# Score masks written to PSUM by VectorE, token sums in two halves and a reordered tail in a recurrent attention kernel

## The chip, the cores and the metric

The kernel runs on one core of one Trainium2 chip. The metric is the time of one execution on the device, in microseconds (us); three runs of the kernel before took 779.76, 780.51 and 783.5 us, so its median is 780.51 us. TensorE is the engine for matrix products (in the profile PE, its weight loads PEld), VectorE is DVE, ScalarE is ACT, GpSimd is POOL, and the queue that issues most transfers is SP.

## What is computed

The output is a gated mixture `g * a + (1 - g) * b` of two branches over 2048 tokens of width 512. Branch `b` is a LayerNorm, a GELU layer of 1376 channels and a second layer back to 512. Branch `a` is attention with a memory that is handed from segment to segment. Cut to what matters:

```python
mem = mem0                                   # 8 rows
for s in range(64):                          # segments of 32 tokens
    h = concatenate([mem, x[32*s : 32*s+32]])      # 40 rows
    q, k, v = (einsum('btd,dhe->bhte', h, W) for W in (Wq, Wk, Wv))   # 32 heads of 128
    scores = einsum('bhqe,bhke->bhqk', q, k) * 128 ** -0.5
    scores = where((row < 8) | (row >= col), scores, -1e9)
    o = einsum('bhqk,bhke->bhqe', softmax(scores), v)
    o = einsum('bhte,hed->btd', o, Wo)
    mem = o[:8]                              # the next segment's memory
    outs.append(o[8:])
```

So segment `s + 1` cannot begin its products with `q`, `k` and `v` before the 8 memory rows of segment `s` have gone through attention and `Wo`.

## The kernel before, in words

**First part.** Up to about 98 us the kernel computes branch `b`, loads the four weight matrices of branch `a`, and builds constants. It ends with the first score mask in PSUM. The mask tile `Mk` holds 0 or -1e9 for four heads, 56 columns a head.

**The loop over segments** (64 segments, four to a tile `T` of 128 tokens, the place in the tile is `si`). The order of the work on each engine is written out by hand in the loop body: an engine carries out its instructions in the order of the source. A tile framework adds a wait wherever one engine's instruction touches what another's has to finish first. The PSUM memory is split into eight tiles of one bank each: `U0` to `U3`, `X1`, `X2`, `SbF` and `W`. The body for one segment is:

1. `qk_unit` (L120): products for Q and K in four passes of 16 matmuls into `U0..U3`; each is cast by ACT (L125) and transposed by DVE (L129) into `QT` or `KT`.
2. `scores(s, 0)` (L257, L261): scores of heads 0 to 15 are added to the mask that stands in `SbF`; ACT takes the exponential of all of them into the first half of `E` (L692).
3. Four passes of V into `X1` (L139), then `mask_mm(1)` (L249): four matmuls with an identity matrix that write the mask into `W`. Then the first pass of the second half of V into `X2`.
4. `msum(0)` (L268, L271): eight matmuls that sum the exponentials of the memory rows over the keys, into a free strip of `U0`. `mnorm(0)`: DVE takes the reciprocal (L688) into 32 columns of `SbF`, and multiplies the memory columns of `E` by it (L689).
5. `scores(s, 1)` onto the mask in `W`; ACT takes the exponentials in two pieces (L681), the memory columns first.
6. Two more passes of V, then `msum(1)` and `mnorm(1)` (its reciprocal lies in `W`), then the last pass of V, which ACT copies out (L710).
7. `run(W1)`: filling work (see below). `xsums` (L600): 16 small matmuls that sum the exponentials of the token rows into `SbF`. `recip_x`: DVE takes their reciprocal (L611), SP writes it to memory and reads it back to all partitions, DVE copies the reciprocals of the memory rows out (L617), and POOL adds them to a running sum (L618).
8. `av` (L281, L286): `E` times V for heads 0 to 15, then for heads 16 to 31, into `U0..U3`. ACT copies the memory rows to `UT` (L718) and the token rows to `XR` (L606).
9. `run(W2)`, then `wo_pass` (L151): 32 matmuls with `Wo` into `W`; ACT casts the result in two halves into `w` (L633).
10. `mask_mm(0)` into `SbF`, `run(W3)`, in some segments an output of an earlier tile (`out_sel`), and `new_mem` (L640, L642): the new memory rows, transposed into the next segment's `hT`.

The filling work is a generator of at most eight steps a segment, each four matmuls of 512 columns (Q, K, V or `Wo` of tokens that do not depend on the memory). `WS` says how many steps stand at the places `W1`, `W2` and `W3`: `(3, 2, 0)` for `si` = 0 and `(2, 2, 2)` for the others; one more stands between the two halves of `new_mem`, and what is left behind them.

**The tail.** The last segment takes no new memory. Its token sums go into `SbF` (`sums`, L268 and L271), DVE takes one reciprocal of 256 columns (L746) and multiplies `E` by it, `av` follows, then `wo_left` (32 matmuls, L151), two reductions that look for bad numbers (L763, L764), `wo_pass`, five selection matmuls (L772, L774), one gated sum (L777) and one output transfer (L778).

Of the kernel before, what the change touches and what calls it, by code (L numbers as in the profile page):

```python
# [10 lines left out]
BF16 = mybir.dt.bfloat16  # L11
# [16 lines left out]
def kernel(ctx, tc, A_x, A_mem0, A_Wq, A_Wk, A_Wv, A_Wo, A_seg_len, B_x, B_w1, B_b1, B_w2, B_b2, gate_w, out):  # L28
# [45 lines left out]
    VP = [ep.tile([P, SPT, 2, Dh], BF16, name=f"VP{i}") for i in range(2)]  # L74
    Mk = ep.tile([P, 4, EW], BF16)
    BO = ep.tile([P, P], BF16)
# [169 lines left out]

    def mask_mm(i2):
        for j in range(4):
            nc.tensor.matmul(Sb[i2][32 * j:32 * j + 32], lhsT=ident[:, 32 * j:32 * j + 32], rhs=Mk[:],  # L249
                             start=True, stop=True, skip_group_check=True, tile_position=(0, 32 * j))  # L250

# [40 lines left out]
    with tc.tile_pool(name="mlpw", bufs=1) as mlpw, \  # L292
# [69 lines left out]
        nc.gpsimd.iota(io[:], pattern=[[1, RIDE]], base=0, channel_multiplier=0)  # L362
        nc.gpsimd.memset(Mk[:], 0.0)

# [196 lines left out]

    mask_mm(0)
    Rs = {}
# [27 lines left out]

    xs8 = SbF[:, 256:256 + NG]
    RW = 9 * NG

    def xsums(s, E):

        for first, c0, n in ((True, 8, 32), (False, 0, LEFT)):
            for i in range(NG):
                c, h = i % 4, i // 4
                nc.tensor.matmul(xs8[32 * c:32 * c + n, 4 * h:4 * h + 4], lhsT=E[:, i, c0:c0 + n], rhs=BO[:, 0:P:32],  # L600
                                 start=first and h == 0, stop=not first, skip_group_check=True, tile_position=(0, 32 * c))

# [6 lines left out]
    def recip_x(s):  # L609
        R = Rs.pop(s)  # L610
        nc.vector.reciprocal(out=R[:, 8 * NG:RW], in_=xs8)  # L611

        Rb = cw.tile([P, P, NG], FP32, tag="Rb", bufs=1, name="Rb")
        nc.sync.dma_start(r_dr[s % 2][:], R[:, 8 * NG:RW])
        nc.sync.dma_start(Rb[:].rearrange("p r e -> p (r e)"), r_dr[s % 2][:].rearrange("r e -> (r e)").partition_broadcast(P))
        for i2 in (1, 0):
            nc.vector.tensor_copy(out=R[:, 32 * i2:32 * i2 + 32], in_=RP[i2])  # L617
        nc.gpsimd.tensor_tensor(out=racc[:, 0:RW], in0=racc[:, 0:RW], in1=R[:, 0:RW], op=ALU.add)  # L618
        Rbs[s] = Rb
# [24 lines left out]

    WS = ((3, 2, 0), (2, 2, 2), (2, 2, 2), (2, 2, 2))
    for s in range(nseg):
# [18 lines left out]
        for n, (t, hf) in enumerate(((0, 0), (1, 0), (0, 1), (1, 1))):  # L665
# [27 lines left out]
        for kc in range(KC):  # L693
            v_unit(X1, hc, 0, kc)
        mask_mm(1)
        nc.scalar.copy(out=v_out(V, 0), in_=X1[:])  # L696
# [12 lines left out]
        v_unit(X2, hc, 1, 3)  # L709
        nc.scalar.copy(out=v_out(V, 1), in_=X2[:])  # L710
        if last:
            break
        run(W1)
        xsums(s, E)
        recip_x(s)
# [7 lines left out]
        if s >= 1:  # L723
            ws[s - 1] = w
        mask_mm(0)
        run(W3)
# [15 lines left out]
    sums(xsum, E, 8, 0, 32, True)  # L742
    for _ in out_sel(T - 1, X2):
        pass
    nc.gpsimd.memset(UL[T % 2][:, :, :, LEFT * si:seg], 0.0)
    nc.vector.reciprocal(out=R[:, nx], in_=SbF[:, 0:32 * NG])  # L746
# [8 lines left out]
    flush(dve_q, 9)  # L755
    for _ in wo_left(T, X1):
# [10 lines left out]
    nc.vector.tensor_scalar(out=good[:, 1:2], in0=tot[:, 1:2], scalar1=RSUM_MAX, scalar2=None, op0=ALU.is_lt)  # L767
    wf = wo_pass(UF)
    nc.tensor.matmul(X1[0:1, 0:1], lhsT=good[:, 0:1], rhs=good[:, 1:2], start=True, stop=True)
    bad = okp.tile([1, 1], I32)  # L770
    nc.vector.tensor_scalar(out=bad[:], in0=X1[0:1, 0:1], scalar1=-1.0, scalar2=float(P), op0=ALU.mult, op1=ALU.add)
    nc.tensor.matmul(X2[:], lhsT=SelL[:], rhs=wls.pop(T)[:], start=True, stop=False, skip_group_check=True)  # L772
    for i in range(SPT):
        nc.tensor.matmul(X2[32 * i:32 * i + 32, :], lhsT=(SelR if i < si else SelI)[:], rhs=(ws.pop(SPT * T + i) if i < si else wf)[:],  # L774
                         start=False, stop=True, skip_group_check=True, tile_position=(0, 32 * i))
    o = cw.tile([P, Dm], BF16, tag="o", name="o")
    nc.vector.scalar_tensor_tensor(out=o[:], in0=X2[:], scalar=g_all[:, T:T + 1], in1=cs.pop(T)[:], op0=ALU.mult, op1=ALU.add)  # L777
    nc.sync.dma_start(out2[T * P:(T + 1) * P, :], o[:])  # L778
    man.__exit__(None, None, None)
# [122 lines left out]
```

## Time and profile before

| What | us |
|---|---|
| Runs of the kernel before | 779.76, 780.51, 783.5 (median 780.51) |
| Profiled execution, its own time | 779.49 |
| Its span, first to last instruction | 777.7 |
| PE busy | 761.1 (98% of the span) |
| ACT busy | 529.5 (68%) |
| DVE busy | 345.1 (44%) |
| POOL busy | 278.7 (36%) |
| Mean granted TensorE clock | 0.997 |

The profile is one execution. A row of its timeline gives the start in us from the span's beginning, the duration, the engine, the line of the kernel, the operation, output and inputs with their sizes, and the number of instructions that the row merges; square brackets give how long the engine sat idle before the row and what ended the wait. Matmuls overlap in a pipeline, so a group of matmuls costs TensorE the distance from its start to the start of the next group, not the duration of its row. A view of waits gives, for each pair of waiting and releasing instruction, the total, the number and the longest.

### The profile page before, as it was taken

To read this page: it belongs to the slowest core of one execution; us is meant where nothing else is said; L and a number is where in the kernel's file an instruction comes from. 1 tells how busy PE (TensorE), PEld (TensorE's weight loads), DVE (VectorE), ACT (ScalarE), POOL (GpSimd) and SP (SyncE) were. 2 spreads that over 40 slices of the span, in tenths; PEclk is the share of its full clock that TensorE was granted. 3 is DMA by queue.
4 is the path that set the end of the run, shared out by engine and by line. 5 is a ranking of instruction groups with operands and counts; after the bars stand their busy time and mean duration, and the time that the engine had idled before them with its cause. 6 is when DMAs were issued, how large, how long until landed. Compare 5 with 4: busy or idle time off the path is not lost.

```text
span 777.7 us, 44316 instructions
## 1 busy us (share of the span) xinstructions
PE 761.1 (98%) x19687; PEld 420.3 (54%) x19687; DVE 345.1 (44%) x1235; ACT 529.5 (68%) x1439; POOL 278.7 (36%) x523
## 2 busy tenths in 40 slices
PE   7999999999999999999999999999999999999996
PEld 5666555555555555555555555555555555555553
DVE  5776254344435343434443443534343444444334
ACT  4666576777777677777777677767777777777663
POOL 4111033433443433344433334434324443343342
PEclk9999999999999999999999999999999999999999
DMA  6779412212122222212221212222231212121221
GB/s 195 271 245 390 139 58 62 75 61 79 62 62 71 79 72 68 80 52 72 62 88 61 89 62 56 67 79 72 71 80 58 70 54 88 62 82 62 66 62 48
DMA packets 53174, 70.61 MB, mean 91 GB/s; under 512 B 21289, under 2 KB 42898, under 8 KB 51442
## 3 DMA queue, kind: packets, MB, share of 16 engines
q1 hardware_dynamic: 51250, 64.84, 26.0%
q8 instruction: 156, 2.56, 1.3%
q0 software_dynamic: 784, 1.97, 0.7%
q10 hardware_dynamic: 944, 0.92, 0.3%
q14 instruction: 40, 0.33, 0.1%
HBM read 56.96 MB, written 4.45 MB: 79 GB/s over the span
## 4 chain that ended last, share of the span: by engine, by line
PE 87%; DVE 1%; ACT 0%; issue 0%; DVEq 0%
PE U L120 29%; PE X L139 18%; PE W L151 15%; PE X L120 8%; PE X L151 4%; PE U L281 3%; PE U L640 2%; PE U L268 1%; PE W L257 1%; PE SbF L257 1%; PE W L249 1%; PE SbF L600 1%; PE SbF L249 1%; PE U L286 1%; PE U L466 1%; PE U L221 0%
## 5 line engine op out<-in xcount | busy, mean ns | idle before, releaser
L626 POOL TENSOR_TENSOR UT<-XR,Rb 128x384 bf16<-128x384 bf16 x126 | 140.1, 1133 | 296.2 <-DMA Rb<-r_dr 215.9
L125 ACT CAST Tb<-U 128x512 bf16<-128x512 f32 x258 | 150.8, 585 | 76.3 <-PE U L120 75.3
L120 PEld LDWEIGHTS <-hT 128*32 128x32 bf16 x4096 | 104.6, 96 | 109.3 <-DVE hT L642 16.3
L139 PE MATMUL X<-Wv_sb,hT 128*32 128x512 bf16 x2048 | 151.2, 379 | 0.0
L120 PE MATMUL U<-Wq_sb,hT 128*32 128x512 bf16 x2048 | 133.3, 380 | 0.5 <-DVE hT L642 0.2
L120 PE MATMUL U<-Wk_sb,hT 128*32 128x512 bf16 x2048 | 132.7, 379 | 0.0
L151 PE MATMUL W<-Wo_sb,UT 128*32 128x512 bf16 x2080 | 125.2, 380 | 1.3 <-ACT UT L718 1.2
L642 DVE CAST hT<-U 128x16 bf16<-128x16 f32 x126 | 21.9, 175 | 206.0 <-PE U L640 198.3
L129 DVE STREAM_TRANSPOSE QT<-Tb 128x256 f32<-128x256 f32 x128 | 57.0, 446 | 80.8 <-ACT Tb L125 80.7
L151 PEld LDWEIGHTS <-UT 128*32 128x32 bf16 x2080 | 59.4, 96 | 55.6 <-issue 16.3
L606 ACT CAST XR<-U 128x256 bf16<-128x256 f32 x252 | 78.6, 438 | 0.0
L129 DVE STREAM_TRANSPOSE KT<-Tb 128x256 f32<-128x256 f32 x128 | 57.0, 446 | 46.2 <-ACT Tb L125 46.0
L633 ACT CAST w<-W 128x256 bf16<-128x256 f32 (+1 forms) x128 | 41.9, 378 | 47.3 <-PE W L151 47.3
L626 POOL TENSOR_TENSOR UL<-XR,Rb 128x128 bf16<-128x128 bf16 x126 | 60.4, 503 | 0.0
L618 POOL TENSOR_TENSOR racc<-racc,R 128x72 f32<-128x72 f32 x63 | 21.2, 337 | 107.1 <-PE U L286 75.0
L139 PEld LDWEIGHTS <-hT 128*32 128x32 bf16 x2048 | 48.2, 94 | 21.0
L718 ACT CAST UT<-U 128x64 bf16<-128x64 f32 x252 | 35.3, 227 | 28.3 <-PE U L286 28.3
L710 ACT CAST V<-X 128x512 bf16<-128x512 f32 x64 | 37.4, 585 | 22.5 <-PE X L139 22.5
L466 PE MATMUL U<-w_sb,hTm 128*128 128x512 bf16 (+1 forms) x176 | 52.7, 383 | 0.0
L460 PEld LDWEIGHTS <-w_sb 128*128 128x128 bf16 (+1 forms) x352 | 34.2, 101 | 20.5 <-issue 3.2
L696 ACT CAST V<-X 128x512 bf16<-128x512 f32 x64 | 37.5, 585 | 9.5 <-PE X L139 1.1
L125 ACT CAST Tb<-X 128x512 bf16<-128x512 f32 x62 | 36.9, 595 | 7.8 <-PE X L120 6.0
(159 smaller groups left out, 1168.4 us busy)
## 6 DMA issues: line engine op xcount, KB each, us to landing
Rb<-r_dr SPq DMA_DIRECT2D x63, 512.0 KB, 3.9
Wv_sb<-in_A_Wv_dram SPq DMA_DIRECT2D x4, 1024.0 KB, 7.5
Wq_sb<-in_A_Wq_dram SPq DMA_DIRECT2D x4, 1024.0 KB, 7.2
Wk_sb<-in_A_Wk_dram SPq DMA_DIRECT2D x4, 1024.0 KB, 9.2
Wo_sb<-in_A_Wo_dram SPq DMA_DIRECT2D x4, 1024.0 KB, 15.1
VP<-VL SPq DMA_DIRECT2D x64, 64.0 KB, 3.2
c<-c_dr SPq DMA_DIRECT2D x16, 128.0 KB, 3.2
out_dram<-o SPq DMA_DIRECT2D x16, 128.0 KB, 2.7
```

Source lines behind the costliest of these rows:

```text
L120: nc.tensor.matmul(bk[32 * j:32 * j + 32, :], lhsT=G[:, kc, :], rhs=W5[t][:, kc, h0:h1, j, :], start=(kc == 0), stop=(kc == KC - 1), tile_ ...
L125: nc.scalar.copy(out=Tb[:], in_=bk.rearrange("p (a b e) -> p a e b", a=8, b=2))
L129: nc.vector.transpose(out=dst[:, 8 * hf:8 * hf + 8, c0:c0 + 32, :].rearrange("p a r b -> p a (r b)").bitcast(FP32), in_=Tb[:].rearrange("p ...
L139: nc.tensor.matmul(bk[32 * j:32 * j + 32, :], lhsT=G[:, kc, :], rhs=Wv5[:, kc, 4 * vb:4 * vb + 4, j, :], start=(kc == 0), stop=(kc == KC - ...
L151: nc.tensor.matmul(bk[32 * c:32 * c + 32, :], lhsT=U_[:, j, i, :], rhs=Wo_sb[:, 4 * i + j, :], start=(n == 0), stop=(n == NW - 1), tile_po ...
L466: nc.tensor.matmul(bp(blk, tt)[:], lhsT=hTm[blk % 2][:rows, fc, tt * P:(tt + 1) * P], rhs=w2_sb[:rows, fc, :], start=(fc == 0), stop=(fc = ...
L606: nc.scalar.copy(out=XR[:, j], in_=U[j][:, 0:NG * 40].rearrange("p (i q) -> p i q", q=40)[:, :, 0:32])
L626: nc.gpsimd.tensor_tensor(out=out[:, :, 4 * h:4 * h + 4, o:o + b - a], in0=XR[:, :, 4 * h:4 * h + 4, a:b], in1=Rb[:, h, :, :, a:b], op=ALU ...
L633: nc.scalar.copy(out=w[:, a:a + Dm // parts], in_=W[:, a:a + Dm // parts])
L696: nc.scalar.copy(out=v_out(V, 0), in_=X1[:])
L710: nc.scalar.copy(out=v_out(V, 1), in_=X2[:])
L718: nc.scalar.copy(out=UT[s % 2][:, j, :, 0:M], in_=U[j][:, 0:NG * 40].rearrange("p (i q) -> p i q", q=40)[:, :, 32:40])
```

## The change

Four things change.

- **Masks.** `mask_mm` (four identity matmuls) becomes `mask_put`: a DVE copy from the mask in SBUF to PSUM. `mask_put(1)` (into `W`) stands behind the first transposition of Q; `mask_put(0)` (into `SbF`) at the end of `recip_x`. The mask tile grows by 8 zero columns, which `mask_put(0)` writes too.
- **Token sums in halves.** `xsums` takes a half `h`. The first half is issued right behind `msum(0)` and `mnorm(0)`, ahead of `scores(s, 1)`; the second stays behind `run(W1)`. The sums lie in the 8 columns that the mask copy has set to zero, so no matmul starts an accumulation.
- **Memory-row sums of the second half.** `msum(1)` and `mnorm(1)` stand behind all passes of V. The filling steps for `si` > 0 become `(2, 1, 3)`.
- **Tail.** `out_sel` writes `X1`; three of the eight steps of `wo_left` (into `X2`) come before `wo_pass`; the last `racc` addition moves from POOL to DVE; the selection matmuls, the gated sum and the output transfer are done in two halves of 256 columns, with the matmuls that do not need the last `w` ahead of it.

```diff
-    def mask_mm(i2):
-        for j in range(4):
-            nc.tensor.matmul(Sb[i2][32 * j:32 * j + 32], lhsT=ident[:, 32 * j:32 * j + 32], rhs=Mk[:],
-                             start=True, stop=True, skip_group_check=True, tile_position=(0, 32 * j))
+    def mask_put(i2):
+        c = 4 * EW + (NG if i2 == 0 else 0)
+        nc.vector.tensor_copy(out=(SbF, W)[i2][:, 0:c], in_=MkF[:, 0:c])
...
-    xs8 = SbF[:, 256:256 + NG]
+    xs8 = SbF[:, 4 * EW:4 * EW + NG]
...
-    def xsums(s, E):
-        for first, c0, n in ((True, 8, 32), (False, 0, LEFT)):
-            for i in range(NG):
-                c, h = i % 4, i // 4
-                nc.tensor.matmul(xs8[32 * c:32 * c + n, 4 * h:4 * h + 4], lhsT=E[:, i, c0:c0 + n], rhs=BO[:, 0:P:32],
-                                 start=first and h == 0, stop=not first, skip_group_check=True, tile_position=(0, 32 * c))
+    def xsums(E, h):
+        for c0, n in ((8, 32), (0, LEFT)):
+            for c in range(4):
+                nc.tensor.matmul(xs8[32 * c:32 * c + n, 4 * h:4 * h + 4], lhsT=E[:, 4 * h + c, c0:c0 + n], rhs=BO[:, 0:P:32],
+                                 start=False, stop=True, skip_group_check=True, tile_position=(0, 32 * c))
...
         for i2 in (1, 0):
             nc.vector.tensor_copy(out=R[:, 32 * i2:32 * i2 + 32], in_=RP[i2])
+        mask_put(0)
...
-    WS = ((3, 2, 0), (2, 2, 2), (2, 2, 2), (2, 2, 2))
+    WS = ((3, 2, 0), (2, 1, 3), (2, 1, 3), (2, 1, 3))
...
             qk_tr(qk_cast(bk[:]), (QT, KT)[t], hf, LEFT * (1 - t))
+            if n == 0:
+                mask_put(1)
...
         for kc in range(KC):
             v_unit(X1, hc, 0, kc)
-        mask_mm(1)
         nc.scalar.copy(out=v_out(V, 0), in_=X1[:])
         v_unit(X2, hc, 1, 0)
         if not last:
             msum(0)
             mnorm(0)
+            xsums(E, 0)
         scores(s, 1)
         for i2 in range(2):
             exps(1, i2)
-        for kc in range(1, 3):
+        for kc in range(1, KC):
             v_unit(X2, hc, 1, kc)
-        if not last:
-            msum(1)
-            mnorm(1)
-        v_unit(X2, hc, 1, 3)
         nc.scalar.copy(out=v_out(V, 1), in_=X2[:])
         if last:
             break
+        msum(1)
+        mnorm(1)
         run(W1)
-        xsums(s, E)
+        xsums(E, 1)
         recip_x(s)
         av(s, V, E)
...
-        mask_mm(0)
         run(W3)
...
-    for _ in out_sel(T - 1, X2):
-        pass
     nc.gpsimd.memset(UL[T % 2][:, :, :, LEFT * si:seg], 0.0)
+    for _ in out_sel(T - 1, X1):
+        pass
+    fill = wo_left(T, X2)
+    run(3)
...
-    nc.gpsimd.tensor_tensor(out=racc[:, nx], in0=racc[:, nx], in1=R[:, nx], op=ALU.add)
+    nc.vector.tensor_tensor(out=racc[:, nx], in0=racc[:, nx], in1=R[:, nx], op=ALU.add)
...
-    wf = wo_pass(UF)
+    wf = wo_pass(UF, 2)
+    halves = ((X1, slice(0, Dm // 2)), (X2, slice(Dm // 2, Dm)))
+    for bk, cc in halves:
+        for i in range(SPT):
+            nc.tensor.matmul(bk[32 * i:32 * i + 32, cc], lhsT=SelL[:, 32 * i:32 * i + 32], rhs=wl[:, cc], start=True, stop=False,
+                             skip_group_check=True, tile_position=(0, 32 * i))
+        for i in range(si):
+            nc.tensor.matmul(bk[32 * i:32 * i + 32, cc], lhsT=SelR[:], rhs=ws[SPT * T + i][:, cc], start=False, stop=True,
+                             skip_group_check=True, tile_position=(0, 32 * i))
...
+    for bk, cc in halves:
+        nc.tensor.matmul(bk[32 * si:32 * si + 32, cc], lhsT=SelI[:], rhs=wf[:, cc], start=False, stop=True,
+                         skip_group_check=True, tile_position=(0, 32 * si))
+        nc.vector.scalar_tensor_tensor(out=o[:, cc], in0=bk[:, cc], scalar=g_all[:, T:T + 1], in1=c[:, cc], op0=ALU.mult, op1=ALU.add)
+        nc.sync.dma_start(out2[T * P:(T + 1) * P, cc], o[:, cc])
```

More of the change, by code (lines that the diff above doesn't have):

```diff
@@ L74 @@
     VP = [ep.tile([P, SPT, 2, Dh], BF16, name=f"VP{i}") for i in range(2)]
-    Mk = ep.tile([P, 4, EW], BF16)
+    MkF = ep.tile([P, 4 * EW + NG], BF16)
+    Mk = MkF[:, 0:4 * EW].rearrange("p (a c) -> p a c", c=EW)
     BO = ep.tile([P, P], BF16)
@@ L362 @@
         nc.gpsimd.iota(io[:], pattern=[[1, RIDE]], base=0, channel_multiplier=0)
-        nc.gpsimd.memset(Mk[:], 0.0)
+        nc.gpsimd.memset(MkF[:], 0.0)
         nc.gpsimd.memset(SelM[:], 0.0)
@@ L617, in recip_x @@
             nc.vector.tensor_copy(out=R[:, 32 * i2:32 * i2 + 32], in_=RP[i2])
+        mask_put(0)
         nc.gpsimd.tensor_tensor(out=racc[:, 0:RW], in0=racc[:, 0:RW], in1=R[:, 0:RW], op=ALU.add)
@@ L724 @@
             ws[s - 1] = w
-        mask_mm(0)
         run(W3)
@@ L755 @@
     flush(dve_q, 9)
-    for _ in wo_left(T, X1):
+    for _ in fill:
         pass
@@ L767 @@
     nc.vector.tensor_scalar(out=good[:, 1:2], in0=tot[:, 1:2], scalar1=RSUM_MAX, scalar2=None, op0=ALU.is_lt)
-    wf = wo_pass(UF)
-    nc.tensor.matmul(X1[0:1, 0:1], lhsT=good[:, 0:1], rhs=good[:, 1:2], start=True, stop=True)
-    bad = okp.tile([1, 1], I32)
[L771 to L775, printed above, removed]
-    o = cw.tile([P, Dm], BF16, tag="o", name="o")
-    nc.vector.scalar_tensor_tensor(out=o[:], in0=X2[:], scalar=g_all[:, T:T + 1], in1=cs.pop(T)[:], op0=ALU.mult, op1=ALU.add)
-    nc.sync.dma_start(out2[T * P:(T + 1) * P, :], o[:])
+    wf = wo_pass(UF, 2)
+    wl, c = wls.pop(T), cs.pop(T)
+    halves = ((X1, slice(0, Dm // 2)), (X2, slice(Dm // 2, Dm)))
[6 more added lines that the diff above has]
+                             skip_group_check=True, tile_position=(0, 32 * i))
+    nc.tensor.matmul(U[0][0:1, 0:1], lhsT=good[:, 0:1], rhs=good[:, 1:2], start=True, stop=True)
+    bad = okp.tile([1, 1], I32)
+    nc.vector.tensor_scalar(out=bad[:], in0=U[0][0:1, 0:1], scalar1=-1.0, scalar2=float(P), op0=ALU.mult, op1=ALU.add)
+    o = cw.tile([P, Dm], BF16, tag="o", name="o")
+    for bk, cc in halves:
[3 more added lines that the diff above has]
+        nc.sync.dma_start(out2[T * P:(T + 1) * P, cc], o[:, cc])
     man.__exit__(None, None, None)
```

2 lines of the change are left out of this document (1 added, 1 removed).

## The prediction, made before the changed kernel had run

> **What bounds the kernel now.** I began with the page, which says how much of the span each engine is busy, then went to the timeline of one segment, engine by engine, and last to the waits. The page's span:
>
> ```profile
> span 777.7 us, 44316 instructions
> ```
>
> The page also has TensorE (PE) busy for nearly all of this span, but its rows overlap, so I read the distance from one group's start to the next. Here is PE in a segment with `si` = 1, from the second mask to `wo_pass`:
>
> ```profile
> 406.57 0.27 PE L249 MATMUL W<-Mk,ident 128*32 128x224 bf16 x4
> 406.67 0.39 PE L139 MATMUL X<-Wv_sb,hT 128*32 128x512 bf16 x4
> 406.88 0.19 PE L268 MATMUL U<-E,BO 128*32 128x32 bf16 x4
> 406.91 0.19 PE L271 MATMUL U<-E,BO 128*32 128x32 bf16 x4
> 406.94 0.27 PE L257 MATMUL W<-QT,KT 128*32 128x40 bf16 x16
> 407.04 0.20 PE L261 MATMUL W<-QT,KL 128*32 128x64 bf16 x4
> 407.07 0.63 PE L139 MATMUL X<-Wv_sb,hT 128*32 128x512 bf16 x8
> 407.64 0.20 PE L268 MATMUL U<-E,BO 128*32 128x32 bf16 x4
> 407.67 0.20 PE L271 MATMUL U<-E,BO 128*32 128x32 bf16 x4
> 407.69 0.40 PE L139 MATMUL X<-Wv_sb,hT 128*32 128x512 bf16 x4
> 407.91 0.62 PE L120 MATMUL X<-Wq_sb,GL 128*32 128x512 bf16 x8
> 408.34 0.27 PE L600 MATMUL SbF<-BO,E 128*32 128x4 bf16 x16
> 408.54 0.27 PE L281 MATMUL U<-E,V 32*128 32x40 bf16 x16
> 408.65 0.19 PE L286 MATMUL U<-E,VP 32*128 32x64 bf16 x4
> 408.78 0.27 PE L281 MATMUL U<-E,V 32*128 32x40 bf16 x16
> 408.89 0.19 PE L286 MATMUL U<-E,VP 32*128 32x64 bf16 x4
> 409.02 0.61 PE L120 MATMUL X<-Wq_sb,GL 128*32 128x512 bf16 x8
> 409.49 1.91 PE L151 MATMUL W<-Wo_sb,UT 128*32 128x512 bf16 x32
> ```
>
> Four matmuls of 512 columns cost 0.215 (407.69 to 407.91 for one group, 407.91 to 408.34 for two). The mask at 406.57 costs 0.10. The eight-matmul row of V at 407.07 should cost 0.43, yet the next group starts 0.57 later: PE waits 0.14 before `msum(1)`. `xsums` costs 0.20. Between the two halves of `av` the first half takes 0.24.
>
> VectorE (DVE) and ScalarE (ACT) beside it, first DVE and then ACT:
>
> ```profile
> 406.42 0.45 DVE L129 STREAM_TRANSPOSE KT<-Tb 128x256 f32<-128x256 f32 x1 [0.37 <-ACT Tb L125]
> 407.24 0.37 DVE L688 RECIPROCAL SbF<-U 128x32 f32<-128x32 f32 x1 [0.38 <-PE U L271]
> 407.64 0.22 DVE L689 TENSOR_TENSOR E<-E,SbF 128x64 bf16<-128x64 bf16 x1
> 407.99 0.37 DVE L688 RECIPROCAL W<-U 128x32 f32<-128x32 f32 x1
> 408.39 0.22 DVE L689 TENSOR_TENSOR E<-E,W 128x64 bf16<-128x64 bf16 x1
> ```
>
> ```profile
> 406.28 0.36 ACT L692 ACTIVATE E<-SbF 128x224 bf16<-128x224 f32 x1
> 406.80 0.58 ACT L696 CAST V<-X 128x512 bf16<-128x512 f32 x1
> 407.37 0.42 ACT L681 ACTIVATE E<-W 128x64 bf16<-128x64 f32 x2
> 408.14 0.58 ACT L710 CAST V<-X 128x512 bf16<-128x512 f32 x1 [0.35 <-PE X L139]
> 409.14 0.56 ACT L718 CAST UT<-U 128x64 bf16<-128x64 f32 x4 [0.41 <-PE U L286]
> ```
>
> These show what holds PE. `msum(1)` at 407.64 follows the first of two exponentials (L681, starting at 407.37). The product of `mnorm(1)` ends at 408.39 + 0.22 = 408.61 and the cast of V at 408.14 + 0.58 = 408.72; the second half of `av` starts at 408.78, 0.06 behind the latter. That is the hand-over I use below. `UT` is copied from 409.14, in four copies of some 0.14 to 0.23 each, and `wo_pass` starts at 409.49, 0.71 after the second half of `av`. So the segment is one chain across PE, ACT and DVE: scores, exponential, sums, reciprocal, product, `av`, copy, `wo_pass`, cast, new memory. Filling work only covers its waits.
>
> The end of the segment, PE and then ACT:
>
> ```profile
> 411.22 0.28 PE L249 MATMUL SbF<-Mk,ident 128*32 128x224 bf16 x4
> 411.31 0.62 PE L120 MATMUL X<-Wk_sb,GL 128*32 128x512 bf16 x8
> 411.88 0.22 PE L640 MATMUL U<-SelM,w 128*32 128x8 bf16 x8
> ```
>
> ```profile
> 411.45 0.65 ACT L633 CAST w<-W 128x256 bf16<-128x256 f32 x2 [0.65 <-PE W L151]
> ```
>
> Behind `wo_pass` PE has the mask (0.09) and two filling steps (0.43), but `new_mem` starts only at 411.88, 0.66 after 411.22. It waits for the first half of the cast that began at 411.45.
>
> **The change, part by part.** The decisive part is a wait. I read the order of the changed program on PE with its waits (here without the weight loads; line 273 is the end of `msum(0)`, 601 is `xsums`, 259 is `scores(s, 1)`):
>
> ```
> L273 Matmult U_106<-E,BO 32x32
> L601 Matmult SbF<-BO,E 32x4 [waits DVE_49]
> L601 Matmult SbF<-BO,E 32x4
> ...
> L259 Matmult W<-QT,KT 32x40
> ```
>
> The value for which this wait stands is the count that DVE reaches with the product of `mnorm(0)` (`E<-E,SbF`, line 693 there). The two do not share a number: the sums read other columns of `E` and write other columns of `SbF` than the 32 that the product reads. But both are in the bank `SbF`. The old `xsums` carried the same wait: its product ended at 407.64 + 0.22 = 407.86, its first matmul ran at 408.34, so the wait cost nothing. Now it stands between `msum(0)` and `scores(s, 1)`, and behind it on PE are queued the second scores, three passes of V, `msum(1)`, the filling work and `av`; ACT waits for those scores with the exponentials, and DVE with `mnorm(1)`.
>
> The Trainium skill, page "PSUM — Partial Sum Buffer", section "PSUM bank collisions raise a hardware error", tells one to guard PSUM by bank and quadrant of partitions, not by address. By that rule the wait is needed and the time is the one forecast below; guarded by address alone it would be the 774 of the first rival. This trace can't show which, since its `xsums` starts after the product anyway.
>
> The new chain from the rows above, for `si` = 1 to 3:
>
> - The mask is gone, so `msum(0)` starts at 406.88 - 0.10 = 406.78. Its exponential ends at 406.28 + 0.36 = 406.64, in time.
> - DVE's reciprocal begins 0.33 after the row 406.91 of `msum(0)`, so at 406.81 + 0.33 = 407.14. The last transposition of K (406.42 + 0.45 = 406.87) is over. Reciprocal to end of product takes 407.24 to 407.86 = 0.62: ended at 407.76.
> - Hand-over 0.06: the first-half sums start at 407.82. PE stands still for about 0.95.
> - Eight sums: half of 0.20 at most. Eight matmuls of `new_mem` take 0.06 (411.88 to the next row at 411.94), which has no change of tile shape behind it; I take 0.06. `scores(s, 1)` starts at 407.88 against 406.94, 0.94 late.
> - Scores 0.13 (406.94 to 407.07), three groups of V 0.65: `msum(1)` at 408.66. The first exponential starts 0.43 after the scores and takes half of 0.42, so it is ready at 408.58, and the old wait of 0.14 is gone.
> - `msum(1)` to the end of its product takes 407.64 to 408.61 = 0.97, with the hand-over 1.03: the second half of `av` can start at 408.66 + 1.03 = 409.69. PE's own work on the way, `msum(1)` 0.05, two filling steps 0.43, sums of the second half 0.16 (0.06 and the 0.10 that the old sums cost above that), first half of `av` 0.14 to 0.24, ends at 409.54 at most, so PE waits here again. Before it was 408.78: the segment is 0.91 late.
> - From there to `wo_pass` 0.71 as before: the copies of `UT` set it, and one filling step less (`W2` from 2 to 1) takes cover away that no row needs. Bounds: 0.05 gained to 0.05 lost.
> - Behind `wo_pass` three steps (0.65) stand where a mask and two (0.52) stood; `new_mem` waits for the cast until 0.66 either way. So the other mask's removal is worth nothing, and neither is `W3`.
>
> For `si` = 0, where `W1` is three steps, the two rows that bound the stretch are these:
>
> ```profile
> 438.64 0.20 PE L268 MATMUL U<-E,BO 128*32 128x32 bf16 x4
> ...
> 439.90 0.28 PE L281 MATMUL U<-E,V 32*128 32x40 bf16 x16
> ```
>
> From the scores to `msum(1)` it is now 0.13 + 0.65 = 0.78 instead of 0.13 + 0.43 + 0.14 = 0.70, so `msum(1)` starts at 438.64 + 0.94 + 0.08 = 439.66. With 1.03 the second half of `av` starts at 440.69 instead of 439.90, 0.79 late. PE's own work on the way (0.05 + 0.65 + 0.16 + 0.14) ends at 440.66.
>
> All this happens in 63 segments (the last has neither `msum` nor `xsums`): 47 x 0.91 + 16 x 0.79 = 42.8 + 12.6 = 55.4.
>
> **The mask copies on DVE.** No row shows a copy into PSUM of 232 columns. The nearest rows bound it: below, the product of 64 columns, 0.22 (407.64); above, a gated sum of 512 columns out of PSUM, mean 749 ns:
>
> ```profile
> L230 DVE SCALAR_TENSOR_TENSOR o<-U,g_all,c 128x512 bf16<-128x512 f32 x14 | 10.5, 749 | 0.0
> ```
>
> By columns 232 lies nearer to the first; I take 0.35. `mask_put(1)` stands ahead of this transposition of K, which the first scores (the second row, PE) need:
>
> ```profile
> 404.69 0.45 DVE L129 STREAM_TRANSPOSE KT<-Tb 128x256 f32<-128x256 f32 x1 [0.36 <-ACT Tb L125]
> ```
>
> ```profile
> 405.58 0.27 PE L257 MATMUL SbF<-QT,KT 128*32 128x40 bf16 x16
> ```
>
> DVE idles 0.36 before it, and it ends at 405.14, 0.44 before those scores. So the copy may take 0.36 + 0.44 - 0.06 = 0.74 and cost nothing. `mask_put(0)` runs after the 8-column reciprocal, which SP's transfer waits for, and after the copies that POOL waits for, so nothing is queued behind it but the cast of new memory, which waits for the matmuls at 411.88, more than 2 us after the copy. I count both as 0.
>
> **The tail.** This row is `wo_left`, eight steps of four matmuls:
>
> ```profile
> 767.43 1.91 PE L151 MATMUL X<-Wo_sb,UL 128*32 128x512 bf16 x32
> ```
>
> Three of the eight steps (3 x 0.215 = 0.65) move ahead, into a stretch where PE waits for the big reciprocal's product; five remain. Working in halves takes part of the last cast, sum and transfer off the end; the addition moved to DVE lengthens the chain of checks there. I take 0.7 gained, with bounds of 1.2 gained and 0.5 lost.
>
> **Sum.** 779.49 (the profiled execution's own time) + 55.4 - 0.7 = 834.2. The median of the runs shown is 1.0 above that execution, so 835.
>
> **The rivals.**
>
> *The wait does not bind.* If the first-half sums ran at once (the product done or the wait released early), `scores(s, 1)` would start at 406.92, held by K's transposition, `msum(1)` at 407.70 behind the third pass of V, `av`'s second half at 408.72, 0.06 early; for `si` = 0, at 438.70 + 1.03 = 439.73, 0.17 early. 47 x 0.06 + 16 x 0.17 + 0.7 = 6.2 gained: 774. It decides if the product ends before 406.84, and the DVE row puts it 0.9 later. For it speaks only that no data passes between the two. Chance 0.04.
>
> *The stall is partly absorbed.* If half of the 0.91 were slack further on, it would be 780.5 + 28 - 0.7 = 808. For it: the later waits at `new_mem` and `av` are waits of PE. Against: their releasers (casts, `mnorm(1)`) stand on the same delayed chain. Chance 0.02.
>
> *The masks bind too.* If the copy took 1.15, K's first transposition would push `scores(s, 0)` by 0.4: 63 x 0.4 = 25 more, 860. The 512-column row at 0.75 speaks against it. Chance 0.03.
>
> **How the numbers follow.** The forecast has 0.91. Its steps are uncertain by about 0.1 a segment (cost of eight sums 0.06 to 0.10, hand-overs, `UT`), 6 us in all; the tail adds 1 and the spread of the runs (779.76 to 783.5) up to 3. That gives 827 to 843, and the rivals outside it hold 0.09. A difference under 0.5% can't be told from none here. Only the first rival is faster, by 0.8%: 0.04. Same needs a mixture: 0.01. Slower: 0.95.
>
> **What would show it.** Right: PE idle for 0.9 ahead of the first-half sums in all 63 segments, released by `E<-E,SbF`; a period about 0.9 longer; no wait left at `msum(1)`, but one of 0.1 to 0.3 before the second half of `av`; mask copies of 0.25 to 0.5 with K's transpositions on time; PE's busy share near 90%. Wrong: first-half sums that start within 0.1 of `msum(0)`, or a segment that makes up the delay before `new_mem`.

## The result: 6.8% slower, as forecast

After the change the kernel takes 834.9 us (median of four runs, 832.08 to 835.48), against 780.46 us for the kernel before on the same chip (779.76 to 783.5). The ratio is 1.0682, with a 95% interval of 1.0663 to 1.0701. The forecast was 835, in a range of 827 to 843.

The profiled execution of the changed kernel took 834.61 us. These lines of its page give the span, the busy time of each engine (us, share of the span, instructions), the shares of the chain of work that ended last, and one group of instructions. In the group's line, the figures behind the bar are its busy time, the mean ns of one, the idle time of PE just before it, and what ended most of that.

```profile
span 832.8 us, 43522 instructions
PE 760.1 (91%) x19173; PEld 426.8 (51%) x19186; DVE 385.7 (46%) x1365; ACT 531.6 (64%) x1440; POOL 277.2 (33%) x522
PE 81%; DVE 5%; POOL 2%; issue 1%; ACT 0%; DVEq 0%
L601 PE MATMUL SbF<-BO,E 128*32 128x4 bf16 x1008 | 27.6, 171 | 50.8 <-DVE E L693 50.8
```

PE has as much work as before (760.1 us against 761.1), but it is 91% of the span instead of 98%. It stands idle for 72.7 us instead of 16.6, and nearly all that was added has one address: 50.8 us ahead of line 601, the token sums, ended by DVE's product `E<-E,SbF` at line 693. The view of waits has the same pair with its number and its longest: it happens in each of the 63 segments that have `xsums`.

```profile
PE SbF L601 <- DVE E L693: 50.8, 63, 0.8
```

Idle time in such a row starts when the last matmul's row ends. The distance from one start to the next is longer, as PE's timeline of one segment with `si` = 1 shows:

```profile
426.92 0.39 PE L122 MATMUL U<-Wq_sb,hT 128*32 128x512 bf16 x4
...
431.58 0.19 PE L270 MATMUL U<-E,BO 128*32 128x32 bf16 x4
431.61 0.19 PE L273 MATMUL U<-E,BO 128*32 128x32 bf16 x4
432.60 0.22 PE L601 MATMUL SbF<-BO,E 128*32 128x4 bf16 x8 [0.81 <-DVE E L693]
432.65 0.28 PE L259 MATMUL W<-QT,KT 128*32 128x40 bf16 x16
...
433.43 0.20 PE L270 MATMUL U<-E,BO 128*32 128x32 bf16 x4
...
433.91 0.22 PE L601 MATMUL SbF<-BO,E 128*32 128x4 bf16 x8
434.06 0.46 PE L283 MATMUL U<-E,V 32*128 32x40 bf16 x16
...
434.50 0.28 PE L283 MATMUL U<-E,V 32*128 32x40 bf16 x16
...
435.21 1.91 PE L153 MATMUL W<-Wo_sb,UT 128*32 128x512 bf16 x32
...
438.18 0.40 PE L122 MATMUL U<-Wq_sb,hT 128*32 128x512 bf16 x4
```

The last part of `msum(0)` starts at 431.61, the first-half sums at 432.60: 0.99 for four matmuls of 32 columns that cost 0.03 in the kernel before (406.91 to 406.94). DVE's timeline beside it holds the cause:

```profile
429.05 0.37 DVE L252 CAST W<-MkF 128x224 f32<-128x224 bf16 x1
429.49 0.45 DVE L131 STREAM_TRANSPOSE KT<-Tb 128x256 f32<-128x256 f32 x1
...
431.93 0.37 DVE L692 RECIPROCAL SbF<-U 128x32 f32<-128x32 f32 x1 [0.27 <-PE U L273]
432.33 0.22 DVE L693 TENSOR_TENSOR E<-E,SbF 128x64 bf16<-128x64 bf16 x1
433.82 0.37 DVE L692 RECIPROCAL W<-U 128x32 f32<-128x32 f32 x1 [1.28 <-PE U L273]
434.23 0.22 DVE L693 TENSOR_TENSOR E<-E,W 128x64 bf16<-128x64 bf16 x1
...
434.75 0.40 DVE L252 CAST SbF<-MkF 128x232 f32<-128x232 bf16 x1
```

The product ends at 432.33 + 0.22 = 432.55, and the sums start 0.05 later. A stretch of the chain that PE once covered with the second scores and V is now bare. The segment lasts from 426.92 to 438.18, 11.26; in the kernel before, the same segment lasted from 402.12 to 412.45, 10.33:

```profile
402.12 0.39 PE L120 MATMUL U<-Wq_sb,hT 128*32 128x512 bf16 x4
...
412.45 0.40 PE L120 MATMUL U<-Wq_sb,hT 128*32 128x512 bf16 x4
```

All 63 periods (the distance between the first Q matmuls of neighbouring segments) taken in this way have these medians, in us:

| Kernel | `si` = 0 | 1 | 2 | 3 |
|---|---|---|---|---|
| before | 10.677 | 10.324 | 10.335 | 10.334 |
| after | 11.461 | 11.264 | 11.276 | 11.275 |

The difference is 0.784 for `si` = 0 and 0.94 for the others: 16 x 0.784 + 47 x 0.94 = 56.7. The segments that are off their median add 3.2 us in all before and 1.7 after, the last segment with the tail is 0.4 shorter, and the first part 0.1 longer. 56.7 - 1.5 - 0.4 + 0.1 = 54.9, and the spans differ by 832.8 - 777.7 = 55.1.

### The profile page after: what moved, and what is told of

It is laid out like the page before. It is cut to its first block, busy times and chain, and to the rows that moved or that the text cites. A ratio compares the mean times of both kernels' runs of the same rounds, so it can differ in the third digit from the quotient of the medians.

```text
span 832.8 us, 43522 instructions
## 1 busy us (share of the span) xinstructions
PE 760.1 (91%) x19173; PEld 426.8 (51%) x19186; DVE 385.7 (46%) x1365; ACT 531.6 (64%) x1440; POOL 277.2 (33%) x522
## 4 chain that ended last, share of the span: by engine, by line
PE 81%; DVE 5%; POOL 2%; issue 1%; ACT 0%; DVEq 0%
PE U L122 27%; PE X L141 16%; PE W L153 15%; PE X L122 6%; PE U L283 4%; PE X L153 3%; DVE SbF L692 3%; PE SbF L601 2%; POOL racc L620 2%; DVE E L693 2%; PE U L642 1%; PE W L259 1%; PE U L288 1%; PE U L273 1%; PE SbF L259 1%
## 5 line engine op out<-in xcount | busy, mean ns | idle before, releaser
L141 PE MATMUL X<-Wv_sb,hT 128*32 128x512 bf16 x2048 | 133.5, 378 | 0.0
L153 PEld LDWEIGHTS <-UT 128*32 128x32 bf16 x2080 | 56.9, 97 | 60.4 <-issue 22.5
L601 PE MATMUL SbF<-BO,E 128*32 128x4 bf16 x1008 | 27.6, 171 | 50.8 <-DVE E L693 50.8
L601 PEld LDWEIGHTS <-E 128*32 128x32 bf16 x1008 | 26.8, 90 | 68.3 <-issue 56.7
L685 ACT ACTIVATE E<-W 128x64 bf16<-128x64 f32 (+1 forms) x128 | 26.8, 262 | 54.4 <-PE W L263 54.4
L692 DVE RECIPROCAL W<-U 128x32 f32<-128x32 f32 x63 | 23.1, 367 | 80.9 <-PE U L273 75.4
L468 PE MATMUL U<-w_sb,hTm 128*128 128x512 bf16 (+1 forms) x163 | 49.5, 381 | 0.6
```

The costliest lines, as they stand in the source:

```text
L141: nc.tensor.matmul(bk[32 * j:32 * j + 32, :], lhsT=G[:, kc, :], rhs=Wv5[:, kc, 4 * vb:4 * vb + 4, j, :], start=(kc == 0), stop=(kc == KC - ...
L153: nc.tensor.matmul(bk[32 * c:32 * c + 32, :], lhsT=U_[:, j, i, :], rhs=Wo_sb[:, 4 * i + j, :], start=(n == 0), stop=(n == NW - 1), tile_po ...
L468: nc.tensor.matmul(bp(blk, tt)[:], lhsT=hTm[blk % 2][:rows, fc, tt * P:(tt + 1) * P], rhs=w2_sb[:rows, fc, :], start=(fc == 0), stop=(fc = ...
L692: nc.vector.reciprocal(out=r, in_=U[i2][:, 320:352])
```

## The experiments

Two theories stood against each other at first. One says that the place of the first-half sums costs all of it, because they must wait for a product with which they share no number, only a PSUM bank (and, in other columns, the tile `E`). The other says that the loss comes from the rest: the mask copies on DVE, the second memory-row sums behind V, or the filling steps. Each time is a median; where an interval is given, the kernel before ran beside it on the same chip (medians of 779.7 to 780.05).

**The reciprocal out of the bank.** `mnorm(0)` writes its reciprocal to SBUF instead of to `SbF`, so its product doesn't touch the bank. The copy that used to bring this reciprocal to SBUF falls away. Everything else is the changed kernel, with the first-half sums in their early place.

```diff
-            r, e = RP[i2], E[:, 4 * i2:4 * i2 + 4, 40:56]...
+            r, e = (R[:, 0:32], RP[1])[i2], E[:, 4 * i2:4 * i2 + 4, 40:56]...
...
-        for i2 in (1, 0):
-            nc.vector.tensor_copy(out=R[:, 32 * i2:32 * i2 + 32], in_=RP[i2])
+        nc.vector.tensor_copy(out=R[:, 32:64], in_=RP[1])
```

> The changed kernel, but the reciprocal of mnorm(0) is written to SBUF (into R) instead of to 32 columns of the PSUM tile SbF, so that VectorE's product no longer touches the bank that the first-half token sums write. Theory (the loss is the wait of the first-half sums for that product, because of the shared bank): the wait goes, scores(s, 1) starts about 4.80 us after the start of the segment instead of 5.73, the period of a segment with si > 0 falls from 11.27 to about 10.27, and the time is 774 (772 to 777). Rival (the loss comes from the mask copies, from the second memory-row sums behind V, or from the filling steps): the time stays above 820.

Measured: 776.62 us (774.74 to 777.17), ratio to before 0.9956 (0.9939 to 0.9974). The 55 us are gone. PE's timeline of a segment with `si` = 1, and the row of the product of `mnorm(1)`:

```profile
404.68 0.19 PE L270 MATMUL U<-E,BO 128*32 128x32 bf16 x4
404.71 0.18 PE L273 MATMUL U<-E,BO 128*32 128x32 bf16 x4
404.73 0.20 PE L601 MATMUL SbF<-BO,E 128*32 128x4 bf16 x8
404.81 0.28 PE L259 MATMUL W<-QT,KT 128*32 128x40 bf16 x16
...
405.60 0.19 PE L270 MATMUL U<-E,BO 128*32 128x32 bf16 x3
...
406.24 0.44 PE L283 MATMUL U<-E,V 32*128 32x40 bf16 x16
...
406.67 0.28 PE L283 MATMUL U<-E,V 32*128 32x40 bf16 x16
```

```profile
406.39 0.22 DVE L692 TENSOR_TENSOR E<-E,W 128x64 bf16<-128x64 bf16 x1
```

The sums start 0.02 after the last group of `msum(0)`, and the second scores 0.08 later. So the early sums as such cost next to nothing. The view of waits names the product by what it writes, `E`, but that is not what the sums wait for: here the product writes the same columns of `E`, and they run at once. The time is 2.6 above the expected 774, though inside its range: the second half of `av` still waits, which the next runs take up.

**Both halves' sums together again.** The changed kernel with the first-half sums back behind `run(W1)`, next to the second half's.

```diff
-            xsums(E, 0)
         scores(s, 1)
...
         run(W1)
+        xsums(E, 0)
         xsums(E, 1)
```

> The changed kernel, but the first half of the token sums stands behind run(W1) again, next to the second half; masks, msum(1) behind V, filling steps and tail as changed. Theory (the place of the first-half sums is the whole loss): no wait of TensorE for the product of mnorm(0), time 775 (773 to 778), within 2 of the version with the reciprocal in SBUF. Rival (the rest of the change costs): above 785.

Measured: 776.54 us, ratio 0.9955 (0.994 to 0.9971). Moving the sums away from the wait and moving the wait away from the sums give the same time. Taken together, DVE's mask copies and the rest of the change don't make the kernel slower.

**The early sums alone.** The kernel before, with its identity matmuls and its old tail, and only `xsums` cut in halves with the first half behind `mnorm(0)`.

```diff
             mnorm(0)
+            xsums(E, 0)
...
-        xsums(s, E)
+        xsums(E, 1)
```

> The kernel before with one part of the change: the first half of the token sums is issued right behind msum(0) and mnorm(0), everything else as before (identity matmuls, msum(1) ahead of the last pass of V). Theory: the sums wait for VectorE's product as in the changed kernel; since the mask is still ahead of msum(0) and the last pass of V stands behind msum(1), a segment loses about 1.04 (si > 0) or 0.92 (si = 0): 47 x 1.04 + 16 x 0.92 = 64, time 844 (838 to 848). Rival (the loss comes from another part): within 5 of 780.

Measured: 839.06 us, in one execution. The periods grow by 0.94 (`si` = 0) and 0.99 (others). The part alone loses more than the whole change: the cause is sufficient as well as necessary.

**A longer product chain.** The changed kernel with the reciprocal of `mnorm(0)` computed twice, one after the other, into the same place.

```diff
             nc.vector.reciprocal(out=r, in_=U[i2][:, 320:352])
+            if i2 == 0:
+                nc.vector.reciprocal(out=r, in_=U[i2][:, 320:352])
```

> The changed kernel with the reciprocal of mnorm(0) computed twice, so that VectorE takes some 0.37 to 0.40 more between msum(0) and the product for which the first-half sums wait. Theory (all of VectorE's chain there is on the path of every segment): 63 x 0.385 = 24 more, 859 (855 to 863). Rival (the stall is partly slack, or something else holds TensorE): below 848.

Measured: 861.89 us, in one execution. The wait of line 601 is now:

```profile
PE SbF L601 <- DVE E L695: 76.8, 63, 1.6
```

Against the 50.8 of the changed kernel that is 26.0 / 63 = 0.41 a segment; the added reciprocal takes 0.37 (row 431.93 above), and the periods grow by 0.40. What DVE takes longer, the segment takes longer: nothing absorbs it.

**The banks exchanged.** In the changed kernel the reciprocal of `mnorm(0)` goes to the bank `W`, that of `mnorm(1)` to `SbF`. The sums still write `SbF`, the second scores `W`. If the wait belongs to the bank, the early sums run at once and the second scores wait; if it belongs to the values or to the order, nothing changes.

```diff
-    RP = [bk[:, 288:320] for bk in (SbF, W)]
+    RP = [bk[:, 288:320] for bk in (W, SbF)]
```

> The changed kernel with the reciprocals of the memory rows in each other's PSUM tile: mnorm(0) uses 32 columns of W, mnorm(1) 32 columns of SbF; no column is written by two. Theory (what counts is the bank, not the columns): the first-half sums run at once, but scores(s, 1), which write W, wait for the product of mnorm(0) instead, and the second-half sums wait for mnorm(1). Against the changed kernel a segment gains the 0.05 of the first-half sums and loses about 0.29, the second-half sums and the first half of av behind the product: 63 x 0.24 = 15 more, 850 (844 to 855). Rival (only the columns of the sums matter): 775.

Measured: 851.89 us, in one execution. PE's timeline of a segment with `si` = 1:

```profile
439.90 0.19 PE L273 MATMUL U<-E,BO 128*32 128x32 bf16 x4
439.93 0.20 PE L601 MATMUL SbF<-BO,E 128*32 128x4 bf16 x8
440.91 0.28 PE L259 MATMUL W<-QT,KT 128*32 128x40 bf16 x16 [0.78 <-DVE E L693]
...
441.74 0.61 PE L122 MATMUL X<-Wq_sb,GL 128*32 128x512 bf16 x8
442.76 0.22 PE L601 MATMUL SbF<-BO,E 128*32 128x4 bf16 x8 [0.40 <-DVE E L693]
```

The same matmuls, on the same columns of `E` and of `SbF`, now start 0.03 after `msum(0)`. The wait has moved to the second scores, whose bank is the one that the product now reads, and a second one stands ahead of the second-half sums, which share `SbF` with the product of `mnorm(1)`: two filling steps and that wait take 442.76 - 441.74 = 1.02, where two steps alone took 0.43. The wait follows the bank.

The wait is an instruction's condition in the program, placed by the framework, which treats each of these tiles of one bank as a unit. The rule of the Trainium skill that the prediction named (page "PSUM — Partial Sum Buffer", section "PSUM bank collisions raise a hardware error") asks for such a guard, and the runs agree with it so far as the program goes: 0.99 with a shared bank, 0.02 without. Whether the chip itself would need this one was not tried, as no run took the wait away and left the bank shared.

**The masks alone.** The kernel before with the mask copies on DVE, at the places of the change, and nothing else.

```diff
         for i2 in (1, 0):
             nc.vector.tensor_copy(out=R[:, 32 * i2:32 * i2 + 32], in_=RP[i2])
+        mask_put(0)
...
+            if n == 0:
+                mask_put(1)
...
-        mask_mm(1)
...
-        mask_mm(0)
         run(W3)
```

> The kernel before with one part of the change: the masks are copied by VectorE instead of the identity matmuls. Theory (the segment is a chain of waits, and the 0.19 us of matmuls lie in its slack): period of a segment 10.31 to 10.33, time 780 (778.5 to 781.5). Rival (TensorE's time is the bound): 63 x 0.19 = 12 less, 768. Rival (the copies delay the transpositions): above 785.

Measured: 775.44 us (774.70 to 775.77), ratio 0.9944 (0.993 to 0.9958). The expectation missed: I had them at nothing, and they are worth 4.6 us, 0.057 in each segment (periods 10.62, 10.267, 10.28, 10.278). PE, then ACT and DVE, of a segment with `si` = 1:

```profile
404.68 0.19 PE L267 MATMUL U<-E,BO 128*32 128x32 bf16 x4
404.71 0.19 PE L270 MATMUL U<-E,BO 128*32 128x32 bf16 x4
404.81 0.28 PE L256 MATMUL W<-QT,KT 128*32 128x40 bf16 x16
...
405.48 0.20 PE L267 MATMUL U<-E,BO 128*32 128x32 bf16 x4
...
406.61 0.46 PE L280 MATMUL U<-E,V 32*128 32x40 bf16 x12
```

```profile
405.20 0.42 ACT L683 ACTIVATE E<-W 128x64 bf16<-128x64 f32 x2
405.97 0.59 ACT L711 CAST V<-X 128x512 bf16<-128x512 f32 x1 [0.35 <-PE X L140]
```

```profile
404.31 0.45 DVE L130 STREAM_TRANSPOSE KT<-Tb 128x256 f32<-128x256 f32 x1 [0.37 <-ACT Tb L126]
```

The mask of 0.10 is off PE and `msum(0)` (404.68) comes that much earlier, but the second scores don't: K's last transposition ends at 404.31 + 0.45 = 404.76, and they start 0.05 behind it. So they follow `msum(0)` by 0.13 instead of 0.06 (406.88 to 406.94), and stand 4.795 behind the segment's start instead of 4.810 (medians for `si` = 1). What moves is behind them: the exponentials start 405.20 - 404.81 = 0.39 after the scores, 0.43 before (407.37 - 406.94). `msum(1)`, the last pass of V, its cast (ended at 405.97 + 0.59 = 406.56) and the second half of `av` (406.61) follow with the same lead. So 0.04 of the gain comes in at the hand-over from the scores to the exponentials, and 0.015 ahead of it. Why that hand-over is shorter was not tried. The periods make 63 x 0.057 = 3.6 of the 4.6 us; the rest has no single place in the profile.

**The late `msum(1)` alone.** The kernel before with `msum(1)` and `mnorm(1)` behind all of V, and the filling steps `(2, 1, 3)`. The masks are identity matmuls, and the sums of both halves stand together.

```diff
-    WS = ((3, 2, 0), (2, 2, 2), (2, 2, 2), (2, 2, 2))
+    WS = ((3, 2, 0), (2, 1, 3), (2, 1, 3), (2, 1, 3))
...
-        for kc in range(1, 3):
+        for kc in range(1, KC):
             v_unit(X2, hc, 1, kc)
-        if not last:
-            msum(1)
-            mnorm(1)
-        v_unit(X2, hc, 1, 3)
         nc.scalar.copy(out=v_out(V, 1), in_=X2[:])
         if last:
             break
+        msum(1)
+        mnorm(1)
```

> The kernel before with msum(1) and mnorm(1) behind all of V and nothing else; masks by identity matmuls, both halves' sums together. The wait of 0.14 at msum(1) goes and a wait of 0.1 to 0.3 ahead of the second half of av may come: periods of 10.32 to 10.34 for si above 0, and 780 (778.5 to 781). If the late msum(1) is worth its old wait in full, 47 x 0.14 = 6.6 less: 774. If it costs the new wait and saves nothing, 63 x 0.2 = 12 more: 792.

Measured: 783.2 us (782.4 to 784.39), ratio 1.0046 (1.003 to 1.0062): slower by 3.5 us and outside my range. Periods 10.553 (`si` = 0), 10.441, 10.452, 10.454: 0.12 shorter in the first segment of a tile and 0.117 longer in the others; 47 x 0.117 - 16 x 0.124 = 3.5. The end of a segment with `si` = 1, PE:

```profile
412.63 0.28 PE L249 MATMUL SbF<-Mk,ident 128*32 128x224 bf16 x4
412.73 0.40 PE L120 MATMUL X<-Wq_sb,GL 128*32 128x512 bf16 x4
412.94 0.62 PE L120 MATMUL X<-Wk_sb,GL 128*32 128x512 bf16 x8
413.37 0.22 PE L640 MATMUL U<-SelM,w 128*32 128x8 bf16 x8
```

With the mask still on PE, three filling steps end at 413.37, 0.74 after the mask's start; `new_mem` could have started at 0.66, as it did before (411.22 to 411.88). This takes 0.08 of the 0.117; the rest was not traced. The new steps `(2, 1, 3)` are free only because the change also takes the mask off PE. The parts of this change aren't independent. My expectation speaks of the late `msum(1)` and "nothing else", but the edit takes the filling steps along, and their cost was left out of it.

**The late `msum(1)` undone.** The first experiment's kernel (reciprocal in SBUF) with `msum(1)` and `mnorm(1)` back ahead of the last pass of V.

```diff
-        for kc in range(1, KC):
+        for kc in range(1, 3):
             v_unit(X2, hc, 1, kc)
+        if not last:
+            msum(1)
+            mnorm(1)
+        v_unit(X2, hc, 1, 3)
```

> The version with the reciprocal in SBUF, and msum(1) with mnorm(1) again ahead of the last pass of V, as in the kernel before. Theory (where the first-half sums don't wait, the second sums behind V cost some 0.06 a segment with si > 0, since mnorm(1) then sets the second half of av; that is why the version with the reciprocal in SBUF has a period of 10.33, the masks alone 10.27): period 10.27 for si > 0, 10.50 for si = 0, time 3 below the version with the reciprocal in SBUF, 773.5 (772 to 775.5). Rival (the place of msum(1) is free): 776 to 777.

Measured: 776.51 us, ratio 0.9951 (0.9932 to 0.9971), no different from 776.62. The expected 3 us didn't come; the rival that calls the place free, with 776 to 777, did. By the periods the place costs 0.02 for `si` above 0 and gains 0.07 for `si` = 0, which nearly cancel (47 x 0.02 = 0.9 against 16 x 0.07 = 1.1). With the masks alone, however, the periods of `si` above 0 are 0.05 shorter still (10.267 against 10.312), and those two kernels place `msum(1)` alike. There the exponentials start 0.03 earlier behind the scores (0.39 against 0.42): the same open hand-over.

**The tail alone.** The kernel before with the changed tail: three steps of `wo_left` ahead of `wo_pass`, the last `racc` addition on DVE, and the end in two halves.

```diff
+    fill = wo_left(T, X2)
+    run(3)
     nc.vector.reciprocal(out=R[:, nx], in_=SbF[:, 0:32 * NG])
...
-    nc.vector.scalar_tensor_tensor(out=o[:], in0=X2[:], ...)
-    nc.sync.dma_start(out2[T * P:(T + 1) * P, :], o[:])
+    for bk, cc in halves:
+        nc.tensor.matmul(bk[32 * si:32 * si + 32, cc], lhsT=SelI[:], rhs=wf[:, cc], ...)
+        nc.vector.scalar_tensor_tensor(out=o[:, cc], in0=bk[:, cc], ...)
+        nc.sync.dma_start(out2[T * P:(T + 1) * P, cc], o[:, cc])
```

> The kernel before with the changed tail alone. Theory of the prediction: 0.7 gained, 779.4 against the kernel before on the same chip at 780.1. From the profile of the changed kernel, whose last segment and tail take 19.7 instead of 20.1: 0.4 gained, 779.7. Rival (the tail costs, by the longer chain of checks on VectorE): 0.5 lost, 780.6.

Measured: 779.6 us, ratio 0.9991 (0.9974 to 1.0007). By the time it can't be told from no change. The profile puts the last segment and the tail at 19.52 us against 20.06.

**The best of the parts.** The kernel of the masks alone, with the changed tail, and `msum(1)` behind V in the first segment of each tile only.

```diff
-        if not last:
+        if not last and si > 0:
             msum(1)
             mnorm(1)
...
+        if si == 0:
+            msum(1)
+            mnorm(1)
```

> The kernel before with the mask copies by DVE, the changed tail, and msum(1) behind V in the first segment of each step alone; the sums of the second half of the tokens stay together with the first. If the price of the change lies in the early first-half sums alone, the rest of it is worth what its parts measured: 780.5 less the 5.0 of the masks' run, less 0.5 for the tail (19.52 against 20.06 in the tail's run), less some 0.07 x 16 = 1.1 in the first segments: 774 (773 to 775.5). Rival: the tail's half microsecond and the first segments' tenth are lost again, so that it stands with the masks' run at 775.4. Rival with the other sign: the tail's two transfers cost more than they save, 776 or above.

Measured: 774.45 us (773.37 to 776.13), ratio 0.9932 (0.9918 to 0.9947): 0.7% faster than before, and 60 us below the changed kernel. Against the masks alone the profile shows shorter first segments (10.521 against 10.62) and a shorter last segment with the tail (19.39 us against 20.24); the two times, 774.45 and 775.44, have overlapping intervals.

## Why the prediction was right, point by point

**The wait.** It is there in 63 segments, with the releaser that the prediction named, and every point of the chain came out within 0.03. Counted from the start of `msum(0)`, which the prediction put at 406.78 and this segment has at 431.58:

| Step | Predicted | Measured |
|---|---|---|
| product of `mnorm(0)` ends | 0.98 | 0.97 |
| first-half sums start | 1.04 | 1.02 |
| `scores(s, 1)` | 1.10 | 1.07 |
| `msum(1)` | 1.88 | 1.85 |
| second half of `av` | 2.91 | 2.92 |
| `wo_pass` | 3.62 | 3.63 |

The agreement at `av` is made of two misses. Up to `msum(1)` the chain was 0.03 quicker than priced, and from `msum(1)` to the second half of `av` it took 434.50 - 433.43 = 1.07 instead of 1.03. The prediction took over the 0.97 that `msum(1)` and its product need when they stand ahead of the last pass of V; behind all of V they take 434.45 - 433.43 = 1.02. Why they do isn't shown.

**The new wait at `av`.** The first half of `av` takes 434.50 - 434.06 = 0.44 instead of 0.14 to 0.24, so PE waits 0.20 to 0.30 for the product of `mnorm(1)` (ended at 434.23 + 0.22 = 434.45), as forecast. The old wait ahead of `msum(1)` is gone: three passes of V take 433.43 - 432.65 = 0.78 with the scores, the sum that the prediction gave.

**The period.** 0.91 and 0.79 were forecast, 0.94 and 0.784 measured. The extra 0.03 for `si` above 0 makes 1.4 us, and the segments off their median, of which the prediction says nothing, took 1.5 off: the two misses cancel. That 834.9 falls on 835 to the tenth is luck; the 0.91 a segment is not.

**The mask copies.** 0.35 us was the price; the rows have 0.37 for the copy of 224 columns into `W` and 0.40 for that of 232 into `SbF`. K's transposition follows 429.05 + 0.37 = 429.42 at 429.49, without harm to the first scores. The rival in which the copies bind would have needed 1.15.

**The masks valued at nothing.** The prediction says this of the mask ahead of `new_mem` only, and inside the changed kernel it is right: the third filling step takes that place. The 0.10 of the other mask it lets through to `msum(0)`, which stands 431.58 - 426.92 = 4.66 behind the segment's start, as forecast. It was the expectation of the masks' run that put both at nothing, and as a statement on the masks by themselves that is wrong: alone they are worth 4.6 us, most of it through the start of the exponentials. It let the mask's 0.10 pass into the old wait ahead of `msum(1)` and didn't ask whether that wait's releaser, the exponential, would come earlier too.

**The tail.** 0.7 was forecast, with bounds of 1.2 gained and 0.5 lost; 0.37 came. Here are the last segment's start, the last cast, the last gated sum and the last transfer's issue, first before, then after:

```profile
757.67 0.40 PE L120 MATMUL U<-Wq_sb,hT 128*32 128x512 bf16 x4
...
771.12 0.58 ACT L633 CAST w<-W 128x512 bf16<-128x512 f32 x1 [1.14 <-PE W L151]
...
772.17 0.75 DVE L777 SCALAR_TENSOR_TENSOR o<-X,g_all,c 128x512 bf16<-128x512 f32 x1 [0.87 <-PE X L774]
772.95 0.34 SPq L778 DMA_DIRECT2D out_dram<-o  x1
```

```profile
813.10 0.40 PE L122 MATMUL U<-Wq_sb,hT 128*32 128x512 bf16 x4
...
825.49 0.65 ACT L635 CAST w<-W 128x256 bf16<-128x256 f32 x2 [1.14 <-PE W L153]
...
826.22 0.88 DVE L789 SCALAR_TENSOR_TENSOR o<-X,g_all,c 128x256 bf16<-128x256 f32 x2
827.10 0.82 SPq L790 DMA_DIRECT2D out_dram<-o  x2
```

The cast starts 771.12 - 757.67 = 13.45 after the segment's start before and 12.39 after, 1.06 earlier. In the run with the changed tail alone it starts 771.49 - 758.69 = 12.80 after it, 0.65 earlier: this is the price that the prediction put on the three steps. Behind the cast, working in halves first gains and then loses. From the cast to the sum it takes 826.22 - 825.49 = 0.73 instead of 1.05; but two half sums take 0.88 instead of 0.75, and two issues 0.82 instead of 0.34. From the cast's start to the end of the issues that makes 2.43 instead of 2.17, so the prediction's "working in halves takes part of the last cast, sum and transfer off the end" holds for the cast alone. From there to the end of the span it is 832.8 - 827.92 = 4.9 instead of 777.7 - 773.29 = 4.4. That is not a price of the second transfer: over the profiles of all runs this last stretch takes 4.3 to 4.9 us with the changed tail (4.3 in the run with it alone) and 4.4 to 4.8 with the old one. So the 0.37 of one profile is not known to better than some tenths.

**The rival without the wait.** Its condition was made true in two ways by the first two experiments, which gave 776.6 and 776.5 where it had 774. K's last transposition does hold the second scores, as it says, and with the reciprocal in SBUF `msum(1)` starts 405.60 - 404.81 = 0.79 behind them, where it had 0.78. The miss lies between `msum(1)` and the second half of `av`: 406.67 - 405.60 = 1.07 instead of 408.72 - 407.70 = 1.02, and 47 x 0.05 is 2.4. It is the same 0.97 as above: here `msum(1)` to the end of its product takes 406.39 + 0.22 - 405.60 = 1.01. The rival in which the stall is partly absorbed is excluded by the doubled reciprocal: 0.37 more in gave 0.40 more out.

## What to carry to other kernels

A matmul moved up in an in-order queue takes its waits along, and all that is queued behind it pays for them, so list the waits that the new place makes real, also those on a tile that is merely shared. Before a small result is put into a spare corner of a PSUM bank, look who else touches that bank at that time: here the same 32 columns cost 55 us in one place and nothing in SBUF. Measure the parts of a change alone as well as together, since a loss of one can hide the gain of another (the masks), and one part can be free only because of another (the filling steps).

## What the runs showed that was not expected

- The exponentials of the second scores start 0.43 us after these scores in the kernel before and 0.39 with the mask copied by DVE, though the scores are the same instructions. This alone carries 0.04 of the 0.057 a segment that the masks are worth. The runs have an order: it is 0.43 where PE goes straight from `msum(0)` to the scores (the kernel before, the late `msum(1)` alone), 0.42 where the early sums fill most of the time until K is transposed (the reciprocal in SBUF), and 0.39 where PE stands still ahead of the scores (the masks alone, the sums together again, and the changed kernel with its long wait). No run varied this pause alone, so the cause stays open.
- Eight sums of 4 columns between `msum(0)` and the second scores cost 404.81 - 404.73 = 0.08, but without them the step from `msum(0)`'s last group to the scores takes as long (404.71 to 404.81 = 0.10 with and without them), because the scores wait for K's last transposition in both: in the place where the wait does not bind, they are free.
- A copy of 128x224 from SBUF to PSUM takes 0.37 us on DVE into `W` and 0.40 into `SbF` (the masks alone), so the 8 more columns are not what makes the copy into `SbF` slower in the changed kernel. Four identity matmuls cost PE 0.10 (0.09 for the other mask). The slower operation wins here, but not by the 0.19 that it takes off PE: all but 0.057 of this goes into waits, that of the second scores for K's transposition and that of `new_mem` for the cast of `w`.
